# A two-layer kernel whose second layer reuses the first layer's tile objects instead of new tiles at the same addresses

## Chip, cores and metric

The kernel runs on one core of a Trainium2 chip. The metric is the device time of one execution in microseconds (us), as a median over runs; lower is better. The traces are of one profiled execution each. Engines: PE is the matmul engine (PEld its weight loads), DVE the vector engine, ACT the scalar engine, POOL and SP the two others (SP issues the DMAs).

## What is computed

Attention over local keys (a window of 16 to either side) and over block summaries (32 tokens each), for 2 batches, 8 heads, 768 tokens, head size 64; then two feed-forward layers on the 1536 tokens of width 512, with 2048 hidden units each. What matters here is the two layers:

```python
h = x @ w_in
g = h * np.clip(h + 3.0, 0.0, 6.0) / 6.0      # layer 0
x = g @ w_out
h = x @ w_in2
g = h * (1.0 / (1.0 + np.exp(-h)))            # layer 1
return g @ w_out2
```

## The kernel before, in words

Every product of a layer is done in split precision: an operand is kept as a rounded part (`hi`) and the rest (`lo`), and three matmuls (hi·hi, hi·lo, lo·hi) make one product. The tokens stand in three blocks `j` of 512. Each layer works through its hidden units in two halves.

The order of the work is written out by hand. `ORDER` is a list of steps; `PROGRAM` goes through it and calls one small function for each step, and a star at a step gives its copy to DVE instead of ACT. Each engine runs its own instructions strictly in that order; the framework adds the semaphore waits, from what it knows of the tiles that an instruction reads and writes. The same bytes of SBUF are used by several tiles in turn, through a pool with one buffer for each `tag`.

Steps that the change and the prediction touch:

- For most hidden units the first product is not made by plain matmuls. Pairs `p` of weight blocks go through a scheme with seven products for eight (as Strassen's), which needs sums of weight blocks and sums of token blocks. `ssum p k` (line 1009, DVE) makes weight sum k, `s_hi p k` (line 1019, ACT or DVE) writes its rounded part and `s_lo p k` (line 1023, DVE) its rest. `prod p k` (line 1041 in `six`, PE) makes product k of pair p; `u2`, `vee`, `u4`, `c22` and others (lines 1083 to 1120) combine the products.
- The rounded and split weight sums have no buffer of their own. They lie in parts of the token tile of block 1 that no product reads as tokens any more: `sb` is made of four slices `x[:, n, b, 0:2, :]` of that tile (line 1017). Product 3 reads the other half of this tile, `[..., 2:4, :]`, as its moving operand, and the slice with n = 1, b = 1 as its stationary one.
- `act i` (line 769, ACT) applies the activation, `gate i` (line 778, DVE) the gate, `gate_hi i` (line 787) and `gate_lo i` (line 793, DVE) split the gated value, `project i part` (lines 813 and 816, PE) makes the second product of the layer.
- `finish 0 1 j m` (line 862, DVE; line 892, ACT) adds the last part of layer 0 to the output sum `acc` and writes the rounded token of layer 1; `finish_lo` (line 900, DVE) writes its rest. `tsumb` and `tsum` (lines 969 and 931) make the token sums of layer 1.
- The tiles: `x1` holds the tokens of layer 0 (blocks 0, 1 and the last, with tags `x0`, `x1` and `late`), `acc` the output sums (tags `ka0`, `ka1`). In layer 1, `second_x(j)` and `acc_part(1, i)` ask the pool for new tiles with the same tags, so that they get the same addresses. A new tile in a used buffer is free when every access to the old tile is done; two accesses to one tile are ordered only where their parts overlap.

Around the change of layers, `ORDER` has this stretch, in which pair 7 is the last of layer 0 and pair 8 the first of layer 1:

```python
prod 7 2, u4 7,
project 39 1, prod 7 3, s_hi 8 3, s_hi 8 1, ssum 8 4, act 47, gate 47, gate_hi 45, prod 7 4, gate_lo 45,
finish 0 1 2 1, finish 0 1 2 2, conv_top 35, act 46, finish 0 1 2 0, s_hi 8 2, tsumb 1 1, finish_lo 2 2,
```

Of the kernel before, what the change touches and what calls it, by code (L numbers as in the profile page):

```python
# [10 lines left out]
F32 = mybir.dt.float32  # L11
F32R = mybir.dt.float32r
# [25 lines left out]
NWIDE = NT // WIDE  # L38
# [314 lines left out]
def attention_moe_kernel(  # L353
# [13 lines left out]
    main = ctx.enter_context(tc.tile_pool(name="main", bufs=1))  # L367
# [7 lines left out]
    x_shape = [P, WIDE // SUB, 2, KD, SUB]  # L375
    x1 = [main.tile(x_shape, F32R, tag=f"x{j}", name=f"x1_{j}") for j in range(NWIDE - 1)]
# [329 lines left out]
    xs = [x1, {}]  # L706
    acc = {}
# [130 lines left out]
    def acc_part(layer, i):  # L838

        big, i0 = divmod(i, NWIDE * KD // 2)  # L840
        if (layer, big) not in acc:
            shape = [P, NWIDE * KD // 2, DM]
            acc[layer, big] = main.tile(shape, F32, tag=f"ka{big}", name=f"acc{layer}{big}")
        return acc[layer, big][:, i0]

    def halves(part):
# [1 line left out]

    def second_x(j):
        if j not in xs[1]:  # L850
            tag = f"x{j}" if j < NWIDE - 1 else "late"
            xs[1][j] = main.tile(x_shape, F32R, tag=tag, name=f"x2_{j}")
        return xs[1][j]

    def gathered(chunk, m):
        ps = banks.use((chunk, m))
        rows, cols = piece(chunk, m)
        part = acc_part(chunk[0], chunk[2] * KD + rows.start // P)[:, cols.start : cols.stop]
        return ps[:, : len(cols)], part, rows, cols
# [20 lines left out]
    def finish(layer, half, j, m):  # L880
        ps, part, rows, cols = gathered((layer, half, j, half), m)
        if half == 0:
            if layer == 0:
                nc.scalar.mul(part, ps, 1.0 / 6.0)
            else:
                nc.scalar.copy(out=part, in_=ps)
        elif layer == 0:
            add_sixth(ps, part)
            if only_in_sums(j, m):
                return  # L890
            n = sub_parts(j, m)
            nc.scalar.copy(out=second_x(j)[:, :n, 0, m], in_=halves(part)[:, :n])
        else:
            nc.vector.tensor_tensor(out=part, in0=ps, in1=part, op=ALU.add)
            r0 = j * WIDE + rows.start
            nc.sync.dma_start(out=out[r0 : r0 + P, cols.start : cols.stop], in_=part)

    def finish_lo(j, m):
        x2, n = xs[1][j], sub_parts(j, m)
        nc.vector.tensor_tensor(  # L900
            out=x2[:, :n, 1, m], in0=halves(acc_part(0, j * KD + m))[:, :n],
            in1=x2[:, :n, 0, m].bitcast(F32), op=ALU.subtract,
        )
# [7 lines left out]
    def tsum(layer, a, n):  # L911

        x, y = OPERANDS[a]
        out = rs.take(("t", layer, a, n), 3 if a < 3 else 2)

        def whole(j, half):
            return acc_part(0, j * KD + 2 * half + n)

        def split(j, half, ab):
            return xs[0][j][:, :, ab, 2 * half + n, :].bitcast(F32)  # L920

        old = None if a % 2 else rs.use(("t", layer, y, n))
        if layer:
            terms = [(out, whole(*x), old if a % 2 == 0 else whole(*y), ALU.subtract)]
        else:
            o = halves(out)
            y = [halves(old)] if a % 2 == 0 else [split(*y, ab) for ab in range(2)]
            terms = [(o, split(*x, 0), y[0], ALU.subtract), (o, o, split(*x, 1), ALU.add)]
            terms += [(o, o, t, ALU.subtract) for t in y[1:]]
        for o, s, t, op in terms:  # L930
            nc.vector.tensor_tensor(out=o, in0=s, in1=t, op=op)
# [41 lines left out]
    def tb_part(layer, a, ab):  # L973
        if a == 1:
            x = second_x(NWIDE - 1) if layer else xs[0][NWIDE - 1]
            return x[:, 1, ab, 0:2, :]
        return tb[a][:, ab]
# [33 lines left out]
    def s_hi(p, k):  # L1011
        if p not in sb.held:
            layer = p // HALF
            if p % HALF == HALF // 2 * (1 - layer):
                assert not sb.held
                x = second_x(1) if layer else xs[0][1]
                sb.free[:] = [[x[:, n, b, 0:2, :] for n in range(2) for b in range(2)]]
            sb.take(p, 8)
        copier("s_hi", p, k)(out=sb.see(p)[k - 1][:, 0], in_=whole_s.use(p)[:, k - 1])
# [130 lines left out]
    late = main.tile([P, 2 * KD * WIDE], F32, tag="late", name="early_units")  # L1150
# [171 lines left out]
```

## Time and profile before

| | us |
|---|---|
| median of 3 runs | 588.94 (588.72 to 590.15) |
| profiled execution, its own time | 590.55 |
| span in its trace | 588.8 |

The profiled execution's time is 1.75 us over its span: what lies before the first and after the last instruction. It is 1.6 us over the median of the runs. A timeline row has the start, the duration, engine, line, operation, what is written and read, shapes, and how many instructions of the kind were merged; in square brackets stands how long the engine sat idle before it and what ended that. A row of several PE matmuls ends when the last result is in place; the next matmul can start before that.

### The profile page before, as it was taken

The page shows a single profiled execution, that of the slowest core. Times are in us where ns is not written, and L with a number is a line of the kernel's source. Part 1 is how long each engine was busy: PE and PEld are TensorE (multiplying, and loading weights), DVE is VectorE, ACT ScalarE, POOL GpSimd, SP SyncE. Part 2 cuts the span into 40 slices and gives each one's busy share as a digit, 9 for nine tenths or more (in the row PEclk, how much of TensorE's full clock was granted, in tenths as well). Part 3 has the DMA queues.
Part 4 walks back from the last instruction along what each step waited for, and adds up shares of the span by engine and source line. Part 5 has one row for each costly group of instructions (what it writes and reads, how often), then busy time and mean ns, then how long its engine had stood idle before and what let it go on. Part 6 is the DMA issues. An engine that isn't in the chain of part 4 may idle for free.

```text
span 588.8 us, 9590 instructions
## 1 busy us (share of the span) xinstructions
PE 572.1 (97%) x3624; PEld 480.9 (82%) x3624; DVE 441.9 (75%) x1009; ACT 253.0 (43%) x625; POOL 77.5 (13%) x98
## 2 busy tenths in 40 slices
PE   8979999999999999999997999999999999999997
PEld 7758788888888888888885878888888898888886
DVE  4898977556859988988969899756667867568454
ACT  3797766443224354413336453441552253214310
POOL 3256235310000000010200211000020100001000
PEclk9999999999999999999998999999999999999999
DMA  9999784412101121321211022220223222111023
GB/s 220 236 196 246 222 183 146 135 26 72 36 2 36 72 71 39 105 67 47 76 63 40 33 71 59 84 73 0 79 101 107 72 71 72 37 36 38 0 86 130
DMA packets 69806, 51.30 MB, mean 87 GB/s; under 512 B 38400, under 2 KB 64256, under 8 KB 69760
## 3 DMA queue, kind: packets, MB, share of 16 engines
q1 hardware_dynamic: 69760, 50.69, 31.8%
q8 instruction: 28, 0.46, 0.3%
q14 instruction: 18, 0.15, 0.1%
HBM read 47.54 MB, written 3.15 MB: 86 GB/s over the span
## 4 chain that ended last, share of the span: by engine, by line
PE 47%; DVE 4%; ACT 1%; issue 1%; ACTq 0%
PE bank L816 22%; PE bank L1041 20%; PE bank L813 5%; DVE acc L862 1%; DVE w L943 0%; DVE r L778 0%; DVE g L793 0%; DVE g L787 0%; DVE bits L423 0%; DVE values L969 0%; ACT L769 0%; DVE x L1023 0%; DVE x L900 0%; ACT r L1078 0%; ACT r L769 0%
## 5 line engine op out<-in xcount | busy, mean ns | idle before, releaser
L813 PE MATMUL bank<-g,w 128*128 128x512 f32 x432 | 106.3, 393 | 3.5 <-DVE g L793 2.2
L816 PE MATMUL bank<-w,g 128*128 128x512 f32 (+1 forms) x441 | 105.5, 385 | 0.0
L813 PEld LDWEIGHTS bank<-g,w 128*128 128x128 f32 x432 | 80.5, 188 | 21.7 <-DVE g L793 3.1
L816 PEld LDWEIGHTS bank<-w,g 128*128 128x128 f32 x441 | 81.2, 188 | 16.3 <-DVE values L1090 0.2
L438 POOL TENSOR_TENSOR w<-bits,w 128x512 fp32r<-128x512 f32 x26 | 35.8, 1379 | 350.1 <-ACT w L434 272.7
L1041 PE MATMUL bank<-w,x 128*128 128x512 f32 (+1 forms) x360 | 74.6, 348 | 1.1 <-ACT r L769 0.9
L1041 PEld LDWEIGHTS bank<-w,x 128*128 128x128 f32 x360 | 59.0, 189 | 10.6 <-ACT r L769 1.3
L1041 PE MATMUL bank<-x,w 128*128 128x512 f32 (+1 forms) x240 | 49.9, 347 | 0.0
L719 PE MATMUL bank<-x,w 128*128 128x512 f32 x192 | 47.7, 396 | 0.2 <-DVE values L778 0.2
L769 ACT ACTIVATE values<-bank 128x512 f32<-128x512 f32 (+1 forms) x54 | 28.0, 529 | 39.6 <-PE bank L1041 24.6
L1041 PEld LDWEIGHTS bank<-x,w 128*128 128x128 f32 x240 | 39.5, 189 | 5.9 <-ACT values L1078 0.2
L423 DVE SCALAR_TENSOR_TENSOR bits<-words,top 128x512 uint32<-128x512 uint32 x47 | 34.3, 730 | 11.4 <-ACT top L414 8.7
L719 PEld LDWEIGHTS bank<-x,w 128*128 128x128 f32 x192 | 35.2, 188 | 7.9 <-issue 0.7
L769 ACT ACTIVATE r<-bank 128x512 f32<-128x512 f32 (+1 forms) x42 | 20.6, 500 | 48.5 <-PE bank L1041 24.4
L813 PE MATMUL bank<-w,w 128*128 128x512 f32 x144 | 37.9, 401 | 0.0
L816 PE MATMUL bank<-w,w 128*128 128x512 f32 (+1 forms) x147 | 36.9, 385 | 0.0
L793 DVE TENSOR_TENSOR g<-values,g 128x512 fp32r<-128x512 f32 x40 | 27.9, 698 | 9.1 <-ACT g L787 8.9
L414 ACT CAST top<-words 128x512 f16<-128x512 bf16 x35 | 27.2, 777 | 13.9 <-DVE bits L423 8.1
L813 PEld LDWEIGHTS bank<-w,w 128*128 128x128 f32 x144 | 27.7, 194 | 5.9
L816 PEld LDWEIGHTS bank<-w,w 128*128 128x128 f32 x147 | 27.3, 188 | 5.6
L1041 PE MATMUL bank<-w,w 128*128 128x256 f32 (+1 forms) x144 | 28.5, 337 | 0.2 <-ACT r L1078 0.2
L1041 PEld LDWEIGHTS bank<-w,w 128*128 128x128 f32 x144 | 23.2, 189 | 3.6 <-ACT r L1078 0.4
(217 smaller groups left out, 951.5 us busy)
## 6 DMA issues: line engine op xcount, KB each, us to landing
words<-in_moe_w_out_dram SPq DMA_DIRECT2D x32, 511.8 KB, 3.3
words<-in_moe_w_in_dram SPq DMA_DIRECT2D x32, 511.0 KB, 3.8
early_w<-in_q_dram SPq DMA_DIRECT2D x12, 256.0 KB, 5.2
out_dram<-acc SPq DMA_DIRECT2D x11, 256.0 KB, 2.0
early_r<-in_v_dram SPq DMA_DIRECT2D x13, 192.0 KB, 4.5
stage<-in_k_dram SPq DMA_DIRECT2D x3, 512.0 KB, 5.6
stage<-in_v_dram SPq DMA_DIRECT2D x3, 512.0 KB, 7.1
early_w<-in_k_dram SPq DMA_DIRECT2D x6, 256.0 KB, 5.1
```

Source lines behind the costliest of these rows:

```text
L414: copier("conv_top", h)(out=top[:, 1], in_=src[:, 2])
L423: nc.vector.scalar_tensor_tensor(out=bitss.take(h, bit_users(h)), in0=rest, scalar=13, in1=tops.use(h).bitcast(U32), op0=ALU.logical_shift ...
L438: eng.tensor_tensor(out=w_half(h, 1), in0=bitss.use(h).bitcast(F32), in1=w_half(h, 0).bitcast(F32), op=ALU.subtract,)
L719: nc.tensor.matmul(ps[:, :n], w[:, a, kk * P : (kk + 1) * P], x[:, o // SUB : (o + n) // SUB, b, kk, :], start=(m == 0), stop=(m == last),)
L769: nc.scalar.activation(out=r[:, cols], in_=ps, **kind)
L793: eng.tensor_tensor(out=g[:, 1, cols], in0=r[:, cols], in1=g[:, 0, cols].bitcast(F32), op=ALU.subtract)
L813: nc.tensor.matmul(ps[:, o : o + n], lhs, g[:, b, shift : shift + n], **flags)
L816: nc.tensor.matmul(ps[:, : len(cols)], g[:, a, rows], rhs, **flags)
L862: nc.vector.scalar_tensor_tensor(out=part, in0=ps, scalar=1.0 / 6.0, in1=part, op0=ALU.mult, op1=ALU.add)
L1041: nc.tensor.matmul(ps, lhs(a, kk), rhs(b, kk), start=start, stop=(i == 5), skip_group_check=on_top)
```

## The change

In layer 1, `second_x` returns the token tile of layer 0 itself, and `acc_part` the output sum tile of layer 0. The addresses are the ones that the new tiles had. The instructions, their order on each engine and their operands' addresses are the same; what the framework knows of them differs, and with it the waits.

```diff
         if (layer, big) not in acc:
             shape = [P, NWIDE * KD // 2, DM]
-            acc[layer, big] = main.tile(shape, F32, tag=f"ka{big}", name=f"acc{layer}{big}")
+            acc[layer, big] = acc.get((0, big)) or main.tile(shape, F32, tag=f"ka{big}", name=f"acc{big}")
         return acc[layer, big][:, i0]
...
     def second_x(j):
         if j not in xs[1]:
-            tag = f"x{j}" if j < NWIDE - 1 else "late"
-            xs[1][j] = main.tile(x_shape, F32R, tag=tag, name=f"x2_{j}")
+
+            xs[1][j] = x1[j]
         return xs[1][j]
```

Where the waits differ: ACT, before the first instruction that writes into a token tile for layer 1. The two L1019 rows are `s_hi 8 3` and `s_hi 8 1`; the next L769 is `act 47`, the L787 `gate_hi 45`, the two L892 belong to `finish 0 1 2 1` and `finish 0 1 2 2`, the second L769 is `act 46`. `PE_49` and `DVE_49` are those engines' semaphores, and `[waits ...]` names what an instruction waits for. Before:

```order
L787 CAST g_92<-values 128x512 [waits PE_49]
L1019 CAST x_1_2921<-words_69 128x256 [waits PE_49]
L1019 CAST x_1_2921<-words_69 128x256
L769 ACTIVATE r_93<-r_1719 128x512 [waits DVE_49]
L787 CAST w_475<-values 128x512 [waits DVE_49]
L892 CAST x_2_2936<-acc_1956 128x256 [waits DVE_49]
L892 CAST x_2_2936<-acc_1956 128x2x256 [waits DVE_49]
L414 CAST top_66<-words_70 128x512 [waits DMAHW7_49,DMAHW6_49]
L769 ACTIVATE r_1719<-bank_72 128x512
```

The same place on ACT after the change:

```order
L787 CAST g_92<-values 128x512 [waits PE_49]
L1019 CAST x_1_65<-words_69 128x256 x2
L769 ACTIVATE r_93<-r_1719 128x512 [waits DVE_49]
L787 CAST w_475<-values 128x512 [waits DVE_49,PE_49]
L892 CAST x_late<-acc_1956 128x256 [waits DVE_49]
L892 CAST x_late<-acc_1956 128x2x256 [waits DVE_49]
L414 CAST top_66<-words_70 128x512 [waits DMAHW7_49,DMAHW6_49]
L769 ACTIVATE r_1719<-bank_72 128x512 [waits PE_49]
```

No instruction has moved; the wait for PE is no longer at the first L1019. That wait was for the last matmul of `prod 7 3`. It now stands at `act 46`, which reads the bank that `prod 7 3` fills, and `gate_hi 45` has a wait of its own for an earlier matmul, the last reader of the buffer that it overwrites; both of these had been covered by the wait at L1019. On DVE, the L793 of `gate_lo 45` loses its wait for PE, which `gate_hi 45` now covers. No other wait of any engine differs, but that two increments of PE's semaphore stand one matmul off.

## Rows read from the trace of the kernel before

**Rows 1.** The page, part 1: busy time, share of the span, instructions of each engine.

```profile
PE 572.1 (97%) x3624; PEld 480.9 (82%) x3624; DVE 441.9 (75%) x1009; ACT 253.0 (43%) x625; POOL 77.5 (13%) x98
```

**Rows 2.** Windows on PE: stretch, its length, PE busy (matmuls), granted clock, DMA share, GB/s.

```profile
303.00:308.30 5.30, 5.30 (x25) 1.00 0.00 0
308.30:319.60 11.30, 7.82 (x32) 1.00 0.05 16
319.60:323.80 4.20, 4.20 (x12) 0.61 0.29 96
...
350.00:585.80 235.80, 235.80 (x1185) 1.00 0.20 65
```

**Rows 3.** The chain that ended last, in order of time: start, us, what.

```profile
305.79 1.37 PE bank L1041 x6
...
319.60 16.66 PE bank L813 x65
```

**Rows 4.** Timeline of ACT around the change of layers.

```profile
307.18 0.71 ACT L1019 CAST x<-words 128x256 fp32r<-128x256 f32 x2 [6.18 <-PE bank L1041]
...
308.34 0.60 ACT L787 CAST w<-values 128x512 fp32r<-128x512 f32 x1
...
312.16 0.58 ACT L769 ACTIVATE r<-bank 128x512 f32<-128x512 f32 x1
...
314.45 1.15 ACT L787 CAST g<-r 128x512 fp32r<-128x512 f32 x2
```

**Rows 5.** Timeline of DVE in the same stretch.

```profile
308.46 0.69 DVE L778 SCALAR_TENSOR_TENSOR r<-r,r 128x512 f32<-128x512 f32 x1 [5.43 <-ACT r L769]
...
309.68 1.88 DVE L862 SCALAR_TENSOR_TENSOR acc<-bank,acc 128x512 f32<-128x512 f32 x3
...
313.73 0.68 DVE L778 SCALAR_TENSOR_TENSOR r<-r,bank 128x512 f32<-128x512 f32 x1
...
315.39 0.69 DVE L793 TENSOR_TENSOR g<-r,g 128x512 fp32r<-128x512 f32 x1
...
318.86 0.69 DVE L793 TENSOR_TENSOR g<-r,g 128x512 fp32r<-128x512 f32 x1
...
320.06 0.69 DVE L793 TENSOR_TENSOR w<-values,w 128x512 fp32r<-128x512 f32 x1
...
338.92 0.42 DVE L1090 TENSOR_TENSOR values<-bank,r 128x256 f32<-128x256 f32 x1 [1.27 <-ACT r L1078]
```

**Rows 6.** Timeline of PE in the same stretch.

```profile
300.18 1.52 PE L813 MATMUL bank<-w,w 128*128 128x512 f32 x6
...
302.90 2.88 PE L813 MATMUL bank<-g,w 128*128 128x512 f32 x12
...
308.34 0.84 PE L813 MATMUL bank<-g,w 128*128 128x512 f32 x3
310.41 0.96 PE L813 MATMUL bank<-g,w 128*128 128x512 f32 x3 [1.23 <-DVE acc L862]
...
312.58 1.52 PE L813 MATMUL bank<-g,w 128*128 128x512 f32 x6
...
315.30 0.39 PE L813 MATMUL bank<-g,w 128*128 128x512 f32 x1
316.13 1.66 PE L813 MATMUL bank<-g,w 128*128 128x512 f32 x6 [0.44 <-DVE g L793]
319.60 1.77 PE L813 MATMUL bank<-g,w 128*128 128x512 f32 x5 [1.81 <-DVE g L793]
321.17 2.76 PE L813 MATMUL bank<-w,w 128*128 128x512 f32 x6
323.73 3.02 PE L813 MATMUL bank<-g,w 128*128 128x512 f32 x12
326.58 1.52 PE L813 MATMUL bank<-w,w 128*128 128x512 f32 x6
```

**Rows 7.** Waits of PE over the whole span: us in total, times, longest.

```profile
PE bank L1041 <- ACT r L769: 0.9, 1, 0.9
```

## The prediction

> **What bounds the kernel now.** I read the page first, then the windows on PE, then the chain of waits, then the timelines of the one stretch where the chain leaves PE. The page has PE busy for 97% of the span and ACT for 43% [rows 1]: taken alone, little is left to win, and least of all by a wait of ACT. The windows tell where the little is. From 350 to 585.8 us PE is busy for all of 235.80 us at the full clock, 2.4 GHz. From 308.3 to 319.6 it is busy for 7.82 of 11.30, and from 319.6 to 323.8 it is busy throughout, but at a granted clock of 0.61 on average, so part of the stretch was at the lower level, 1.2 GHz [rows 2]. The chain names what stands there: six matmuls of `prod 7 3` end at 307.16, ACT and DVE carry the chain until 319.60, and from there PE has it again [rows 3].
>
> On ACT, the first L1019 sits idle for 6.18 us until those six matmuls are done: ACT was free at 301.00 [rows 4]. The instruction writes one slice of the token tile of block 1; `prod 7 3` reads other slices. DVE waits 5.43 us, from 303.03 to 308.46, for `act 47`, which stands two places behind L1019 on ACT [rows 5]. PE then waits for DVE three times: 1.23, 0.44 and 1.81 us [rows 6]. So a wait of a little used engine is on the path here.
>
> **What the change does.** It removes no instruction, adds none and moves none. It takes one wait away, and two that it had covered come out. The other four tiles (token blocks 0 and last, both output sums) lose or gain no wait, so they cost and give nothing.
>
> **How much PE loses now.** Twelve matmuls from 312.58 to 315.30 take 2.72, or 0.2267 us each, without a gap (six of one row, six of the next step) [rows 6]. By that pitch, from start to start:
> - 308.34 to 310.41: 2.07 for 3 matmuls (0.68), 1.39 lost.
> - 310.41 to 312.58: 2.17 for 9 (2.04; three of the row, six of the next step), 0.13 lost.
> - 315.30 to 316.13: 0.83 for 1 (0.23), 0.60 lost.
> - 316.13 to 319.60: 3.47 for 6 (1.36), 2.11 lost.
> - 319.60 to 321.17, 1.57 for 5 (1.13); to 323.73, 2.56 for 6 (1.36); to 326.58, 2.85 for 12 (2.72): 0.44 + 1.20 + 0.13 = 1.77 lost. This is the low clock; nothing was waited for.
>
> The first four are 4.23 of waiting, the last 1.77 of clock. Check: 54 matmuls need 12.24, 18.24 were taken, 6.00 were lost.
>
> **Where the stall goes.** ACT runs both L1019 and `act 47` from 301.00; these took 1.16 (307.18 to 308.34), so `gate_hi 45` can start at 302.16. Its new wait is for the six matmuls that started at 300.18 and were done after 1.52, at 301.70 [rows 6]: it costs nothing, with 0.46 to spare. DVE goes on at 303.03 and does `gate 47` and `gate_lo 45` in the 1.22 that they took before (308.46 to 309.68), until 304.25. Its first L862 needs the bank that the sixth of the twelve matmuls from 302.90 fills: 302.90 + 6 × 0.2267 + 0.16 (the 2.88 of the row less 12 × 0.2267) = 304.42. So L862 starts at some 304.45 instead of 309.68, **5.2 us earlier**, and DVE's own queue behind it moves by as much.
>
> `act 46` has the wait that L1019 had, for 307.16: before it ran at 312.16 [rows 4], now at 307.18. That is 5.0 earlier, and DVE's `gate 46`, at 313.73 before, comes at 308.5 and finds it done by 307.8. What is queued behind `act 46` on ACT has its inputs from DVE later than that.
>
> Now PE, without gaps from 308.34. I price each place at which it waited, and the one that comes next:
> - 316.13: 25 matmuls on, 314.01. The L793 of 315.39 is over at 315.39 − 5.2 + 0.69 = 310.9: 3.1 to spare.
> - 319.60: 31 on, 315.37. Here a new lateness appears: the second L787 of 314.45 overwrites a buffer whose last readers are the six matmuls of 312.58, now done at 308.34 + 12 × 0.2267 + 1.52 = 312.58. ACT does it until some 313.2. The L793 of 318.86 comes at 313.66 and is done at 314.35: 1.0 to spare.
> - 321.17: 36 on, 316.50. The buffer of this L787 is free six matmuls later, at 313.94; the L793 of 320.06 comes at 314.86 and is done at 315.55: 0.9 to spare.
>
> So all three waits go, and 4.23 with them. The low clock came behind PE's three gaps and not before, and the stretch ahead of them, without gaps, has a clock of 1.00, as has the one from 350 on [rows 2], so I count the 1.77 as gone too.
>
> **Does it stay?** PE is then 6.0 early at 326.58, DVE 5.2. Until the chain runs from PE over DVE again, DVE may be up to 0.8 late for PE; but at 338.92 DVE had waited 1.27 for a copy of a PE result [rows 5], so it has that much spare, and I take nothing off. The 0.9 that PE waits once for an L769 of ACT [rows 7] lies behind that place and moves along, since that chain begins with PE's own result. From 350 on PE is full, and a full engine that starts earlier ends earlier. Weight loads are issued when DVE frees a buffer and move with DVE.
>
> **The sum.** 590.55 − 4.2 − 1.8 = 584.5 against the profiled execution's own time. This stands 1.6 above the median of the runs, nearly the price of the low clock. If the median run does not have that drop, it loses 4.2 and ends at 584.7; if it has, it loses 6.0 and ends at 582.9. The Trainium skill (TensorE: Matmul & The Clock Gate, the part on the HAM clock gate) says that the point at which the clock changes is not tied to the kernel's start and varies from run to run. By that rule, the drop need not be in every run; no trace here but one shows it. I take 584.5. Ends of the one unknown price, the clock: nothing given back, or all.
>
> **Rivals.**
> - *Only part of it comes.* For: two of the spares are 1.0 and 0.9 us, and the PE end times that they use are modelled; a gap may stay, and the low clock with it, or come with the 0.9 us gap of [rows 7]. Against: from the end of the six matmuls to ACT's start lie 0.02 us [rows 3, 4], so a spare of 0.9 is wide. Time: 590.55 − 4.2 = 586.3.
> - *Nothing comes.* ACT is busy for 43%, PE for 97%; the wait for `prod 7 3` is still there, seven instructions later, and could hold up the same chain. Then 588.9. The Trainium skill (Perfetto Trace Analysis, Identifying the Most-Contended Engine) says to improve the engine with the highest occupancy first. By that rule, ACT's wait would be worth nothing; the chain in this trace speaks against it, as it runs through ACT for those microseconds. That the change does nothing at all is excluded by the waits in the order.
> - *Slower.* The gaps go, but the activity of PE differs, and the clock falls elsewhere for longer: at the layer change, where the gap of 0.9 stays. The drop here cost 1.77. From 584.5 to slower than before by 0.3%, 590.7, it needs 6.2, or three and a half such drops; it decides only if some 14 us are run at 1.2 GHz. It would end at some 591. Against: in the trace that gap is followed by 235.8 us at 1.00.
>
> **How the numbers follow.** Forecast 0.71 (584.5, by itself 582.6 to 585.3); part 0.21 (586.3); nothing 0.06 (588.9); slower 0.02 (591). About 0.3%, 1.8 us, is what a measurement of this kernel can tell from no change; the first two cases are both beyond it. The range reaches from the case with the drop in every run (582.9, less the 0.2 by which the runs' lowest stands under their median, and as much again) to the part case and 0.5 more: 582.4 to 586.8.
>
> **What would show it.** Right: no idle of ACT before the first L1019, and some for PE before the second L769 until the same six matmuls; DVE's 5.4 us wait for `act 47` gone; no PE wait for DVE between 300 and 330; a granted clock of 1.00 there; the last chain on PE from before 305 to the layer change; the stretch after it of the same length, 6 us earlier. Wrong: a PE wait for L793 or L862 of about a microsecond in the stretch, a clock below 1.00 there or behind the layer change, or a longer stretch between 338 and 350, which would give the gain back.

## The result, and the profile after

| | before | after |
|---|---|---|
| median of 4 runs, us | 588.83 (588.44 to 590.15) | 584.07 (583.89 to 584.12) |
| profiled execution, us | 590.55 | 584.12 |
| its span, us | 588.8 | 582.4 |

The ratio is 0.9915, with a 95% interval of 0.9898 to 0.9932: 4.8 us less, where 584.5 was forecast. The interval excludes 1 and also 0.997, the 0.3% that the prediction takes for the least that can be told from no change.

The page, part 1, of the changed kernel; it answers to [rows 1]:

```profile
PE 569.7 (98%) x3624; PEld 480.4 (82%) x3624; DVE 442.0 (76%) x1009; ACT 252.8 (43%) x625; POOL 76.6 (13%) x98
```

The same instructions, the same busy time on DVE, ACT and the weight loads. PE's busy time is 2.4 us less with the same matmuls: that is not work saved, but the clock, for the kernel before has 569.7 too in an execution without the low clock (below). The windows on PE of the changed kernel (stretch, length, busy, clock, DMA share, GB/s), against [rows 2]:

```profile
303.00:308.30 5.30, 5.30 (x25) 1.00 0.00 0
308.30:319.60 11.30, 11.30 (x52) 1.00 0.27 91
319.60:323.80 4.20, 4.20 (x21) 1.00 0.02 8
323.80:344.00 20.20, 19.07 (x106) 1.00 0.08 27
344.00:579.40 235.40, 235.36 (x1183) 1.00 0.20 65
```

Where PE was busy for 7.82 of 11.30 us it is now busy throughout, and the clock is 1.00 everywhere. The last window, like that of [rows 2] from 350 on, is full at the clock of 1.00. The chain that ended last says the same of the change of layers; from 301.28 it is on PE until 332.01, where in [rows 3] ACT and DVE had it from 307.16 to 319.60:

```profile
302.64 2.72 PE bank L813 x12
305.36 2.72 PE bank L1041 x12
308.08 21.76 PE bank L813 x96
329.84 2.17 PE bank L1041 x18
```

The timeline of ACT, against [rows 4]:

```profile
299.96 0.63 ACT L787 CAST g<-values 128x512 fp32r<-128x512 f32 x1 [1.07 <-PE bank L813]
300.49 0.71 ACT L1019 CAST x<-words 128x256 fp32r<-128x256 f32 x2
301.10 0.63 ACT L769 ACTIVATE r<-r 128x512 f32<-128x512 f32 x1
301.63 0.61 ACT L787 CAST w<-values 128x512 fp32r<-128x512 f32 x1
304.76 0.41 ACT L892 CAST x_late<-acc 128x256 fp32r<-128x256 f32 x1 [2.52 <-DVE acc L862]
...
305.97 0.77 ACT L414 CAST top<-words 128x512 f16<-128x512 bf16 x1
306.76 0.60 ACT L769 ACTIVATE r<-bank 128x512 f32<-128x512 f32 x1
...
312.20 0.63 ACT L787 CAST g<-r 128x512 fp32r<-128x512 f32 x1 [2.45 <-PE bank L813]
```

The idle time of 6.18 before the first L1019 is gone. ACT still idles, 2.52 and 2.45 us, but now it is early and waits for others. The timeline of DVE, against [rows 5]; its last row is the one at 338.92 there:

```profile
302.45 0.69 DVE L778 SCALAR_TENSOR_TENSOR r<-r,r 128x512 f32<-128x512 f32 x1
303.06 0.69 DVE L793 TENSOR_TENSOR w<-values,w 128x512 fp32r<-128x512 f32 x1
304.04 1.97 DVE L862 SCALAR_TENSOR_TENSOR acc<-bank,acc 128x512 f32<-128x512 f32 x3 [0.29 <-PE bank L813]
...
313.32 0.69 DVE L793 TENSOR_TENSOR g<-r,g 128x512 fp32r<-128x512 f32 x1
...
314.52 0.69 DVE L793 TENSOR_TENSOR w<-values,w 128x512 fp32r<-128x512 f32 x1
...
332.49 0.42 DVE L1090 TENSOR_TENSOR values<-bank,r 128x256 f32<-128x256 f32 x1 [1.27 <-ACT r L1078]
```

And of PE, against [rows 6], now without a gap:

```profile
305.20 1.52 PE L1041 MATMUL bank<-x 128*128 128x512 f32 x6
306.56 1.52 PE L1041 MATMUL bank<-w,w 128*128 128x512 f32 x6
307.92 1.52 PE L813 MATMUL bank<-g,w 128*128 128x512 f32 x6
...
313.36 2.88 PE L813 MATMUL bank<-g,w 128*128 128x512 f32 x12
316.08 1.52 PE L813 MATMUL bank<-w,w 128*128 128x512 f32 x6
```

The same matmul, the first of the row at 308.34 in [rows 6], starts at 307.92 here: this execution came to the place 0.42 us earlier. I take that for chance: the order of instructions and the waits of PE up to there are alike, and two executions of one kernel (with 12 casts, below) stand 1.25 us apart here. To keep such offsets out, I measure below from this matmul to the end of the span, the **rest**. Before it is 588.8 − 308.34 = 280.5, after 582.4 − 307.92 = 274.5: 6.0 less. From the L1090 on, both take the same time, 588.8 − 338.92 = 249.9 and 582.4 − 332.49 = 249.9, so the gain of the layer change is kept to the end.

### The profile page after: what moved, and what is told of

Read it like the earlier page. It is cut to its first block, busy times and chain, and to the rows that moved or that the text cites. A ratio compares the mean times of both kernels' runs of the same rounds, so it can differ in the third digit from the quotient of the medians.

```text
span 582.4 us, 9590 instructions
## 1 busy us (share of the span) xinstructions
PE 569.7 (98%) x3624; PEld 480.4 (82%) x3624; DVE 442.0 (76%) x1009; ACT 252.8 (43%) x625; POOL 76.6 (13%) x98
## 4 chain that ended last, share of the span: by engine, by line
PE 48%; DVE 2%; ACT 1%; issue 0%; ACTq 0%
PE bank L816 23%; PE bank L1041 20%; PE bank L813 6%; DVE w L943 0%; DVE g L787 0%; ACT L769 0%; DVE r L778 0%; DVE acc L862 0%; DVE x L1023 0%; ACT r L1078 0%; DVE bank L1083 0%; DVE r L931 0%; DVE bits L423 0%; DVE g L793 0%; ACT w L940 0%
## 5 line engine op out<-in xcount | busy, mean ns | idle before, releaser
L813 PE MATMUL bank<-g,w 128*128 128x512 f32 x432 | 105.0, 391 | 0.0
L719 PE MATMUL bank<-x,w 128*128 128x512 f32 x192 | 47.7, 396 | 0.6 <-DVE values L778 0.6
L769 ACT ACTIVATE values<-bank 128x512 f32<-128x512 f32 (+1 forms) x54 | 28.0, 529 | 40.4 <-PE bank L1041 24.8
L719 PEld LDWEIGHTS bank<-x,w 128*128 128x128 f32 x192 | 35.2, 188 | 8.3 <-issue 1.1
L769 ACT ACTIVATE r<-bank 128x512 f32<-128x512 f32 (+1 forms) x42 | 20.6, 500 | 48.5 <-PE bank L1041 24.5
L813 PE MATMUL bank<-w,w 128*128 128x512 f32 x144 | 36.6, 391 | 0.0
L1041 PE MATMUL bank<-x,w 128*128 128x512 f32 x144 | 36.4, 391 | 0.0
L793 DVE TENSOR_TENSOR g<-values,g 128x512 fp32r<-128x512 f32 x40 | 27.9, 698 | 8.4 <-ACT g L787 8.2
L414 ACT CAST top<-words 128x512 f16<-128x512 bf16 x35 | 27.2, 777 | 12.3 <-DVE bits L423 6.4
L816 PEld LDWEIGHTS bank<-w,w 128*128 128x128 f32 x147 | 27.4, 188 | 5.5
L813 PEld LDWEIGHTS bank<-w,w 128*128 128x128 f32 x144 | 26.9, 188 | 5.5
L1041 PEld LDWEIGHTS bank<-x,w 128*128 128x128 f32 x144 | 26.5, 188 | 5.3 <-ACT values L1078 0.2
L787 ACT CAST g<-r 128x512 fp32r<-128x512 f32 x21 | 13.0, 620 | 32.7 <-PE bank L816 20.0
```

Source lines behind the costliest of these rows:

```text
L414: copier("conv_top", h)(out=top[:, 1], in_=src[:, 2])
L719: nc.tensor.matmul(ps[:, :n], w[:, a, kk * P : (kk + 1) * P], x[:, o // SUB : (o + n) // SUB, b, kk, :], start=(m == 0), stop=(m == last),)
L769: nc.scalar.activation(out=r[:, cols], in_=ps, **kind)
L787: copier("gate_hi", i)(out=g[:, 0, cols], in_=value(i)[:, cols])
L793: eng.tensor_tensor(out=g[:, 1, cols], in0=r[:, cols], in1=g[:, 0, cols].bitcast(F32), op=ALU.subtract)
L813: nc.tensor.matmul(ps[:, o : o + n], lhs, g[:, b, shift : shift + n], **flags)
```

## The experiments

**Which tile.** First the kernel before, with the old tile kept for block 1 alone (line numbers of the two kernels are the same):

```diff
-            xs[1][j] = main.tile(x_shape, F32R, tag=tag, name=f"x2_{j}")
+            xs[1][j] = x1[j] if j == 1 else main.tile(x_shape, F32R, tag=tag, name=f"x2_{j}")
```

> The kernel before, with one tile kept: the token tile of block 1. If the whole effect is the one wait at the first L1019 (theory), the time is that of the changed kernel, 584.1, with no PE wait for DVE at the change of layers. If the other four tiles carry a part (rival), it lies between 584.1 and 588.8.

Measured: 583.41 (583.08 to 584.12), ratio 0.9901 (0.9873 to 0.9929) to the kernel before in the same job. No PE wait for DVE at the layer change, and a rest of 581.5 − 307.04 = 274.5, that of the changed kernel. The row of PE from which it is taken, with no gap behind it:

```profile
307.04 1.52 PE L813 MATMUL bank<-g,w 128*128 128x512 f32 x6
```

Then the opposite, the changed kernel with a new tile for block 1 alone:

```diff
-            xs[1][j] = x1[j]
+            xs[1][j] = main.tile(x_shape, F32R, tag="x1", name="x2_1") if j == 1 else x1[j]
```

> The changed kernel, with a new tile for block 1 alone; the four other tiles are kept. Theory: the time of the kernel before, 588.8, with the idle of 6.2 us before the first L1019 and PE's three gaps. Rival (the other tiles carry a part): under 588.

Measured: 588.93 (587.65 to 590.68), ratio 0.9998 (0.9983 to 1.0013). The timelines of ACT and of PE of this kernel:

```profile
307.37 0.72 ACT L1019 CAST x<-words 128x256 fp32r<-128x256 f32 x2 [6.18 <-PE bank L1041]
```

```profile
310.60 0.96 PE L813 MATMUL bank<-g,w 128*128 128x512 f32 x3 [1.23 <-DVE acc L862]
...
316.31 1.65 PE L813 MATMUL bank<-g,w 128*128 128x512 f32 x6 [0.43 <-DVE g L793]
319.79 1.76 PE L813 MATMUL bank<-g,w 128*128 128x512 f32 x5 [1.82 <-DVE g L793]
```

All of the stall is back: PE's three waits and ACT's idle time agree with [rows 4, 6] to 0.01 us. So one of the five tiles carries the whole effect; for the other four no effect is seen, as forecast, and the interval leaves room for under 0.2%.

**The wait, or what stands behind it.** In the kernel before, with all its new tiles and its wait, the two casts go behind `gate_hi 45`:

```diff
-project 39 1, prod 7 3, s_hi 8 3, s_hi 8 1, ssum 8 4, act 47, gate 47, gate_hi 45, prod 7 4, gate_lo 45,
+project 39 1, prod 7 3, act 47, gate 47, gate_hi 45, s_hi 8 3, s_hi 8 1, ssum 8 4, prod 7 4, gate_lo 45,
```

> The kernel before with all its new tiles and its wait, but the two L1019 (and ssum 8 4 on DVE) stand behind act 47, gate 47 and gate_hi 45 in the order. Theory (what cost time is not the wait but what was queued behind it on ACT): ACT still idles until the end of prod 7 3, at the L1019, but act 47 and gate_hi 45 are done by then. The L892 behind it come at about 307.8 instead of 305.2, so DVE loses some 1.8 of the 5.2 us that it gained, 0.9 more than the smallest spare: about 585.0, with one PE gap of about 1 us. Rival (a wait of ACT for the end of prod 7 3 costs its length wherever it stands): 588.8.

Measured: 585.48 (584.51 to 585.68), ratio 0.993 (0.9906 to 0.9954). Its timelines of ACT, of DVE and of PE:

```profile
300.85 0.62 ACT L769 ACTIVATE r<-r 128x512 f32<-128x512 f32 x1
301.68 0.62 ACT L787 CAST w<-values 128x512 fp32r<-128x512 f32 x1 [0.21 <-PE bank L813]
307.12 0.71 ACT L1019 CAST x<-words 128x256 fp32r<-128x256 f32 x2 [4.82 <-PE bank L1041]
307.74 0.92 ACT L892 CAST x<-acc 128x256 fp32r<-128x256 f32 x2
```

```profile
308.69 1.03 DVE L900 TENSOR_TENSOR x<-acc,x 128x512 fp32r<-128x512 f32 x2 [1.60 <-ACT x L892]
```

```profile
308.27 1.52 PE L813 MATMUL bank<-g,w 128*128 128x512 f32 x6
...
316.17 1.45 PE L813 MATMUL bank<-g,w 128*128 128x512 f32 x5 [0.70 <-DVE g L793]
```

ACT still waits 4.82 us for the end of `prod 7 3`, at the same instruction, but most of the loss is gone: the rest is 583.8 − 308.27 = 275.5, 1.0 over the changed kernel, where 0.9 was worked out. The wait itself is cheap. What cost most of the time was `act 47` and `gate_hi 45`, whose inputs were there, in the queue behind it. What is left comes from the two L892, which still stand behind the wait: DVE waits 1.60 us for them, and one PE wait of 0.70 follows. `ssum 8 4` moved on DVE too, but DVE still comes early to its first L862 and waits there for PE (0.16 us).

**How much lateness is free.** In the changed kernel the first cast is repeated 4, 8 and 12 times, each repetition after the one before it, so that ACT comes later by a chosen amount (lines from 1021 on move by 4):

```diff
-prod 7 3, s_hi 8 3, s_hi 8 1,
+prod 7 3, s_hi 8 3, linger 4, s_hi 8 1,
...
+    def linger(n):
+        for _ in range(n):
+            nc.scalar.copy(out=sb.see(8)[2][:, 0], in_=whole_s.see(8)[:, 2])
```

> The changed kernel, with the first L1019 done four times more on ACT, one after the other, some 0.42 us each, so that act 47 and gate_hi 45 come 1.7 us later. Theory: DVE had 0.8 us to spare for act 47 and PE 0.9 to 1.0 for DVE, so little or nothing is lost: 584.1 to 584.8, and the clock stays at 1.00. Rival (the end moves with ACT's delay): 585.8.

> The same with eight, 3.4 us later. Theory: the spares of 0.8 and about 1 are used up, and 1.3 to 1.6 us are lost, at the place where PE waited 1.81 before (g for the L813 of that row): 585.4 to 585.7 while the clock stays at 1.00. If a gap of that size already takes the clock down: 587. Rival (no dependence on the delay): 584.1.

> The same with twelve, 5.0 us later, nearly what the wait cost before. Theory: PE has all three gaps again, 3 to 5 us in total, and the low clock behind them in the profiled execution or not: 587 to 590. Rival: 584.1.

| extra casts | they take, us | median, us | ratio to before | PE's waits at the layer change for DVE | rest |
|---|---|---|---|---|---|
| 4 | 1.72 | 584.12 (583.78 to 584.57) | 0.9917 (0.9900 to 0.9934) | none | 582.0 − 307.58 = 274.4 |
| 8 | 3.47 | 585.84 (585.06 to 586.47) | 0.9949 (0.9931 to 0.9966) | 1.31 | 584.1 − 308.05 = 276.1 |
| 12 | 5.23 | 587.43 (586.85 to 588.82) | 0.9981 (0.9971 to 0.9992) | 0.21, 0.43, 1.80 | 585.1 − 307.31 = 277.8 |

The first 1.7 us are free; of the next 1.75, 1.6 are paid, and of the last 1.76, 1.7. So the changed kernel has about 1.9 us of room on ACT here (5.23 less the 3.3 that they cost). The rows of the changed kernel add up to it: `act 47` is done at 301.73 and DVE comes to its gate at 302.45, 0.72; DVE then waits 0.29 for PE before L862; and PE has 0.9 to spare for DVE (worked out under "Why the prediction was right"). The wait of 6.2 us cost 4.3 (below); the rest was room. The medians with 4 and 12 casts lie in the ranges that were forecast, the one with 8 is 0.14 above its range; its wait of 1.31 stands where it was expected.

The PE timelines of the kernels with 8 and with 12:

```profile
316.55 1.43 PE L813 MATMUL bank<-g,w 128*128 128x512 f32 x5 [1.31 <-DVE g L793]
```

```profile
308.36 0.96 PE L813 MATMUL bank<-g,w 128*128 128x512 f32 x3 [0.21 <-DVE acc L862]
...
314.08 1.66 PE L813 MATMUL bank<-g,w 128*128 128x512 f32 x6 [0.43 <-DVE g L793]
317.55 1.41 PE L813 MATMUL bank<-g,w 128*128 128x512 f32 x5 [1.80 <-DVE g L793]
```

**Is the low clock in every execution?** The kernel before, unchanged, was profiled three times more, and the one with 12 casts once more.

> The kernel before, unchanged, profiled once more. The same stalls are expected in every execution (6.2 us on ACT, 4.2 on PE). If the low clock behind them comes in some executions and not in others (theory), some of these three have a granted clock of 1.00 between 308 and 326 us and a time near 588.8 or below, others 0.6 there and near 590.5. If it comes every time (rival), all three have it and end at about 590.5.

> As the run before it: the kernel before, unchanged, for the clock alone. A granted clock of 1.00 and 588.8 or less, or 0.6 and about 590.5.

> As the two runs before it: the kernel before, unchanged, for the clock alone. A granted clock of 1.00 and 588.8 or less, or 0.6 and about 590.5.

> The changed kernel with twelve extra casts, profiled once more: its first profile had PE's three gaps at a clock of 1.00 throughout and 586.85 us. Theory (the clock falls in some executions): either the same again, or a low clock behind the gaps and about 588.5. Rival (it never falls here, as the gaps are a microsecond smaller in total): 586.9 to 587.5.

Measured, the kernel before: 590.00, 588.33 and 590.47 us. The windows on PE of the first of these executions:

```profile
308.30:319.60 11.30, 7.82 (x32) 1.00 0.09 31
319.60:323.80 4.20, 4.20 (x13) 0.59 0.28 81
```

and of the second, with PE's first row of the stretch:

```profile
307.82 0.84 PE L813 MATMUL bank<-g,w 128*128 128x512 f32 x3
```

```profile
308.30:319.60 11.30, 7.82 (x32) 1.00 0.10 29
319.60:323.80 4.20, 4.20 (x20) 1.00 0.32 96
```

PE is busy for 7.82 us of the stretch with the gaps in both, and its waits are the same (1.23, 0.43, 1.83), but behind them the granted clock is 0.59 in the one and 1.00 in the other. The third has 0.67. The rest of the second is 586.6 − 307.82 = 278.8, against 280.5 in [rows 2, 6]: the low clock costs 1.7, the waits 278.8 − 274.5 = 4.3.

The second execution with 12 casts took 589.74, with nearly the same three gaps (0.20, 0.39, 1.81) and this row in the windows on PE (the first one had 1.00 there and 586.85):

```profile
319.60:323.80 4.20, 4.20 (x13) 0.59 0.30 83
```

It is 588.0 − 308.56 = 279.4 for the rest, 1.6 more than the first one. The other 1.25 of the 2.9 us between the two stand ahead of the layer change (307.31 and 308.56), which is why 588.5 was missed. So of five profiled executions with the stall of the kernel before (these three, [rows 2], and the kernel with a new tile for block 1), four have the low clock, and of two with 12 casts one. That it falls in some executions and not in others is shown; why in these and not in those is not.

Four of five is not the share in all runs. Nearly every execution (not the four runs of the kernel before in the table of the result) has its mean clock over the whole span on record: it is 0.997 in each of the five profiled ones with the drop and 1.000 in the profiled ones without. By that figure, 12 of 34 executions of the kernel before have the drop, 3 of 10 with a new tile for block 1, and 3 of 11 with 12 casts; in the 26 of the kernels with one of PE's three gaps or none, no mean is under 0.999. So by that figure it comes in about a third of the executions with all three gaps, and most runs of the kernel before do not have it. Where in a run the clock fell is read only from the profiled ones.

**A faster version.** Behind the layer change PE keeps the wait of 0.9 us for ACT of [rows 7]. In the changed kernel's trace, ACT there loads its table for Silu for 1.28 us between two instructions of the chain, and had idled 3.24 us shortly before. A Silu on a tile of 128x4 that nobody reads afterwards, placed ahead of the `finish` before which ACT idles, takes the load there (lines from 771 on move by 4):

```diff
+    def silu():
+        t = sts.free[0]
+        nc.scalar.activation(out=t[:, 0], in_=t[:, 0], func=AF.Silu)
...
-finish 0 1 0 2, prod 8 6
+silu, finish 0 1 0 2, prod 8 6
```

> The changed kernel, with a Silu on a spent 128x4 tile ahead of the last finish of layer 0 on ACT, where ACT idles 3.2 us; ACT's load of the activation table, 1.28 us on the chain behind the layer change, then lies in that idle time. If the gap of 0.9 us that PE has left there is set by the table load (theory), the gap goes and the time is 583.1 to 583.3. If the gap is set by DVE's chain (rival), 584.1.

Measured: 582.94 (582.31 to 583.30), just under the forecast, ratio 0.9888 (0.9867 to 0.9909). The timelines of ACT and of PE in the changed kernel:

```profile
339.07 0.62 ACT L892 CAST x<-acc 128x512 fp32r<-128x512 f32 x1 [3.24 <-DVE acc L862]
...
340.72 1.28 ACT L769 ACT_TABLE_LOAD   x1
342.01 0.38 ACT L769 ACTIVATE r<-bank 128x256 f32<-128x256 f32 x1
```

```profile
342.45 1.67 PE L1041 MATMUL bank<-w,x 128*128 128x512 f32 x6 [0.91 <-ACT r L769]
```

and in this one:

```profile
335.70 1.28 ACT L773 ACT_TABLE_LOAD   x1
336.99 0.21 ACT L773 ACTIVATE stat<-stat 128x4 f32<-128x4 f32 x1
338.93 0.62 ACT L896 CAST x<-acc 128x512 fp32r<-128x512 f32 x1 [1.73 <-DVE acc L866]
```

```profile
338.50 4.27 PE L1045 MATMUL bank<-w,x 128*128 128x512 f32 x18
```

PE's wait of 0.9 is gone: these 18 matmuls, the last six of which are those that had waited, run as one row. The rest is 581.2 − 307.77 = 273.4, 1.0 less than in the changed kernel. The median is 0.5 under the 583.41 of the kernel with block 1 alone, which ran beside it, but the runs of the two overlap; executions begin the stretch more than a microsecond apart, so the rest, of one execution each, is the better measure (274.4 to 274.5 in the three kernels that keep the 0.9 and have no other gap here). This version has the lowest median of all that were run.

## Why the prediction was right

- **The bound.** A wait of ACT, busy for 43%, was on the path, and the chain of waits showed it. The experiments with the tile of block 1 agree in both directions.
- **The sum.** 4.23 of waiting and 1.77 of clock were worked out; 4.3 and 1.7 were measured, by the executions with and without the low clock. The whole, 6.00, is the 6.0 of the two profiled executions.
- **The start of the gated work.** `gate_hi 45` was forecast 6.18 us earlier in its execution and L862 5.2; with the offset of 0.42 taken out they came 308.34 − 301.63 − 0.42 = 6.3 and 309.68 − 304.04 − 0.42 = 5.2 earlier.
- **The spares.** 1.0 and 0.9 us were forecast. In the changed kernel the L793 at 313.32 is done at 314.01, and PE needs it with the eighth matmul of the row at 313.36, at 313.36 + 7 × 0.2267 = 314.95: 0.94. The L793 at 314.52 is done at 315.21, for the row at 316.08: 0.87. The series of casts shows the same room from outside.
- **A new wait that was not seen.** I expected ACT to idle before the second L769, which took over the wait for `prod 7 3`. It has none: L414 keeps ACT until 306.74, and the six matmuls are over at 305.20 + 1.52 = 306.72. The wait is there and costs nothing, by chance of an instruction in front of it.
- **That it stays.** DVE's 5.2 against PE's 6.0 did no harm, as the 1.27 that DVE had waited before L1090 [rows 5] promised: L1090 still waits 1.27 in the changed kernel, and it comes 338.92 − 332.49 − 0.42 = 6.0 earlier. Nothing was given back behind it (249.9 us to the end in both).
- **The median.** 584.5 starts from a profiled execution with the low clock, which stood 1.6 above the median, and takes the clock's 1.77 off again. So it says nearly the same as the prediction's 584.7 for a median run without the drop, and that is the case that holds: of 29 runs of the kernel before, made beside the experiments, 21 have a mean clock of 1.00 and a median of 588.5, and eight have 0.997 and 589.5. From 588.5 to 584.07 are 4.4, about the 4.3 of the waits; the 4.8 between the two medians above is 0.5 more than that, which the spread at the start of the stretch can cover, but whether it does isn't shown. The kernel before spreads over 587.65 to 590.94 in 15 runs, the changed one over 583.89 to 584.12 in 4. That the own time of the profiled execution came out at 584.12 and not at 584.55 is the offset of 0.42.
- **A slip that cost nothing.** In the rival "slower", 6.2 us lost at half the clock are some 12 us at 1.2 GHz, not 14; the sum and the range do not use it.

The Trainium skill (TensorE: Matmul & The Clock Gate, the part on the HAM clock gate) says that the point at which the clock changes varies from run to run. The profiles of the unchanged kernel, with 0.59, 0.67 and 1.00 behind equal gaps, go further: whether it falls at all varies. By the rule of the Trainium skill's Perfetto Trace Analysis (Identifying the Most-Contended Engine), the engine with the highest occupancy comes first, with other measures than matmul busy time for TensorE. Here PE has the highest, and what its gaps waited for stood in the queue of an engine with 43%, worth 0.8% of the time. The rule does not say that such a wait is worth nothing; that was the prediction's reading in its second rival, and the trace decides against it.

## What to carry to other kernels

When a buffer is handed on part by part, keep the same tile: a new tile at the same address waits for every access to the old one, also to parts that it doesn't touch yet. What a wait costs is not its own length: it is how much it delays ready work behind it in the same queue, less what the consumers of that work have to spare. Here 6.2 us of waiting cost 4.3, and 4.8 us of it in a better place cost 1.0. Search a chain for places where it leaves the busy engine, however idle the engine is to which it goes.

## What was not expected of the hardware

Equal gaps on PE (7.8 to 8.0 us busy in the windows' 11.30, no single wait over 1.83) were followed by the low level of the clock, 1.2 GHz, in four profiled executions of five and by the full one in the fifth, which is of the same program as three of the others; it costs 1.6 to 1.7 us each time. With 12 casts it fell in one execution of two, with 8.89 busy of 11.30 where it fell and 9.01 where it did not. Over all executions it is about a third, by the mean clocks. The profiles of the kernels with one of these gaps or none have 1.00 here. And two executions of the same program come to the same matmul 1.25 us apart (307.31 and 308.56, with 12 casts), which is why single times were not compared.
